# Attention with relative bias and a maxout FFN: row pairs from (2,3) on, and DMA transposes of q and k at later places

## The chip, the cores and the metric

The kernel runs on one core of a Trainium2 chip. The core has a matrix engine (TensorE, PE in the profile; its weight loads are PEld), a vector engine (VectorE, DVE), an activation engine (ScalarE, ACT), GpSimd (POOL), SyncE (SP), which issues transfers, and 16 DMA engines, which carry out what SP, POOL and ACT issue. The engines run their instructions in order, each by itself, and wait for one another by semaphores. The metric is the time of one execution on the device, in microseconds (us); less is better.

## The reference

```python
batch, n_heads, seq, head_dim = (8, 8, 576, 64)
scores = scale * np.matmul(q, k.transpose(0, 1, 3, 2))
scores = scores + bias.transpose(2, 0, 1)[None, :, :, :]   # bias by distance, 32 buckets
attn = np.exp(scores - max); attn = attn / (sum + 1e-09)
x = np.matmul(attn, v)  ->  (4608, 512): tokens x all heads
h = np.maximum(np.maximum(x @ w1, x @ w2), x @ w3)         # 512 -> 768
out = h @ w_out                                            # 768 -> 512
```

Eight batches of eight heads, 576 tokens each, give 4608 tokens of 512 numbers; each goes through three products, their maximum, and one product more.

## The kernel before

**Visits.** The kernel works through batch indices b = 0 to 7 and, in each, through four head pairs hp = 0 to 3; one step (b,hp) is called a visit here. A visit computes the scores of its two heads transposed, keys on the 128 partitions: four key tiles of 128 (tiles `sc`), and the 64 left-over keys and queries (`sct`, `scq`). ScalarE takes the exponential into `e` (main) and `el` (left over), and VectorE multiplies by a band of exponentials of the bias (`hank`, `bandt`). The weighted sum over v (tile `a`) of a visit stands in the next visit, since its exponentials have to be there; VectorE divides it by the sums (`rd`, `x_sb`). After the last head pair of a batch five DMA transposes bring `x_sb` into `xT`, as the FFN needs it.

**The FFN beside it.** The FFN of 512 tokens is cut into stages, one for each of four visits: from (b,2) on, (b,2), (b,3) and (b+1,0) each compute the first two products for two of six blocks of 128 hidden units and the third product of the two blocks before; (b+1,1) computes three of four output tiles, (b+1,2) the fourth. For batch indices below 2 and in the end the FFN is woven in otherwise.

**Two forms of a visit.** In a *plain* visit (tiled, but not rows) scores come in groups of 256 columns, the left-over keys and the weighted sum use the whole array (128 rows), and the gates use two 64-row tiles with a bank for each output. In a *row* visit everything is made of pairs of matmuls on the two 64-row halves of the array, in two passes with the operands swapped (`rows(False)`, `rows(True)`), with tiles two banks wide; the second pass waits for a semaphore that the end of the first raises. Scores come as `key_scores` of 512 columns, one key tile at a time, and the first one of a visit is computed at the end of the visit before (`ahead`). The constant ROWS (line 64) says with which visit the row form begins. There the banks are allotted anew (lines 1219 to 1223) and the visit computes its first two key tiles itself (`lead`, line 1232). The stages of the FFN of batch b - 1 are planned at (b,1) with the same constant (line 1348): the form of a stage is that of its visit.

**Loads and transposes.** GpSimd's queue loads q and k with a cast to bf16, by head pair: pairs 0 and 1 and the left-over rows of batch b + 2 at the end of (b,1) (`begin_qk`, line 1361), pairs 2 and 3 of b + 1 and its v just ahead of them. From batch 2 on, SyncE's queue transposes them into `qT` and `kT` by DMA, five steps a batch of two transposes (q and k) each: pair 0, the left-over rows (`left`, out of `qtail` and `ktail`), pairs 1, 2 and 3. The function `transposes` (line 724) gives this list; the table `places` (lines 1198 to 1200) says at which place (b, hp, half of the visit) each is put into SyncE's program, and `turn_ahead` (line 1202) does it. The same queue carries the output stores (`store_outputs`) and the transposes of `x_sb` (line 1021), in program order. qT, kT and the load tiles have two buffers, for alternate batches.

A name's first part says what it is in the profile: `psp` are gates, thirds and outputs in pairs of halves, `ps` in the whole array, `pso` outputs, `m` and `hT` the running maximum, `osb` an output tile. All matmuls are recorded at line 109; exponentials at 827; DMA transposes of q and k at 731 (pairs) and 738 (left-over rows).

Of the kernel before, what the change touches and what calls it, by code (L numbers as in the profile page):

```python
# [39 lines left out]
def kernel(  # L40
# [20 lines left out]
    QS = 2 * P  # L61
    QM = 2 * QS
    KT = 4
    ROWS = (3, 0)
    DEEP = 6
    PACKETS = 6 * QM
    FCH = d_ff // P
# [32 lines left out]
    def free_banks():  # L100
        ps_f.release()
        ps_a.release()
# [1094 lines left out]
    turns = {n: [] for n in range(2, B)}  # L1197
    places = {2: ((1, 1, 0), (1, 1, 1), (1, 2, 0), (1, 3, 1), (2, 1, 0)), 3: ((2, 2, 0), (2, 2, 1), (2, 3, 0), (3, 0, 0), (3, 0, 1))}
    for n in range(4, B):
        places[n] = tuple((n - 1, hp, half) for hp, half in ((1, 0), (1, 1), (2, 0), (2, 1), (3, 0)))  # L1200

    def turn_ahead(*place):

# [7 lines left out]
    for b, hp in [(b, hp) for b in range(1, B) for hp in range(HP)]:  # L1211
# [5 lines left out]
        tiled = bool(stages)  # L1217
        rows = (b, hp) >= ROWS
        if (b, hp) == ROWS:
            free_banks()  # L1220
# [124 lines left out]
        if hp == 1 and b > 1:  # L1345
            pending.extend((n, [fn]) for n, fn in rest)
            rest.clear()
            made, tail = ffn((b - 1) * CH, CH, False, [(b + (i + 2) // HP, (i + 2) % HP) >= ROWS for i in range(HP)])
        if hp == 1 and b + 1 < B:
# [23 lines left out]
        if hp == 1 and b > 1:  # L1373
            stages.extend(made)
            strict.append(b)
        if ROWS <= divmod(HP * b + hp + 1, HP) < (B, 0):
            late.append(lambda b=b, hp=hp, e4=e4, el=el: attend_rows(b, hp, e4, el))
# [53 lines left out]
```

## Time and profile before

| | us |
|---|---|
| median of 3 runs | 306.69 |
| lowest and highest run | 306.29, 310.19 |
| span of the profiled execution | 305.2 |
| idle time of TensorE from 88.20 to 96.63 (visit (3,0)) | 8.43 - 8.01 = 0.42 |
| the same from 151.91 to 159.70 (visit (5,0)) | 0.00 |

The profile is of one execution; its own time as a run is not recorded beside its span, from its first instruction to its last. Views used here are the page (busy time of each engine, and the span in 40 slices, each digit the busy share in tenths), the chain of work that ended last (start, duration, what), the waits by engine (total, times, longest) and the timeline: start, duration, engine, line, operation, output<-inputs, form, count, and in brackets the idle time before it with what ended it. A q behind an engine's name is its queue: the instruction only issues a transfer, which lands later. "64*128" in a matmul's form is a half of the array, "128*128" the whole.

### The profile page before, as it was taken

How to read it: one execution, taken by the hardware profiler on the slowest of the kernel's cores; microseconds unless marked ns; L12 is line 12 of the kernel's file. 1: busy time of each engine (PE TensorE's matmuls, PEld its weight loads, DVE VectorE, ACT ScalarE, POOL GpSimd, SP SyncE). 2: the span in 40 equal slices, each digit the busy share in tenths (PEclk: the TensorE clock that was granted, in tenths of full speed). 3: DMA queues.
4: the chain of work that ended last, by engine and by line, in shares of the span. 5: the costliest groups of instructions: out<-in, count | busy, mean ns of one | idle time of the engine just before them, and what ended most of it. 6: DMA issues, size and time to landing. Idle time of an engine off the chain costs nothing.

```text
span 305.2 us, 11001 instructions
## 1 busy us (share of the span) xinstructions
PE 295.5 (97%) x4745; PEld 183.7 (60%) x4745; DVE 206.3 (68%) x455; ACT 201.3 (66%) x270; POOL 143.7 (47%) x199
## 2 busy tenths in 40 slices
PE   8789999999999999999999999999999999999995
PEld 2367877765656676567666766676667654444442
DVE  6489888777776677676777677767776765453552
ACT  3999988977786787768776877677777720222211
POOL 8989677725839746774676469462000000000000
PEclk9999999999999999999999999999999999999999
DMA  9999999999999999999999999999623013202003
GB/s 160 187 203 194 176 137 120 114 165 128 223 150 121 150 131 205 174 143 192 181 139 135 202 162 146 138 197 171 79 46 140 6 40 94 84 0 108 31 0 137
DMA packets 165776, 40.51 MB, mean 133 GB/s; under 512 B 154584, under 2 KB 161248, under 8 KB 165728
## 3 DMA queue, kind: packets, MB, share of 16 engines
q0 software_dynamic: 105664, 16.66, 95.5%
q1 hardware_dynamic: 58304, 22.69, 41.6%
q8 instruction: 37, 0.61, 0.8%
q10 hardware_dynamic: 1760, 0.47, 0.7%
q14 instruction: 11, 0.09, 0.1%
HBM read 35.39 MB, written 9.45 MB: 147 GB/s over the span
## 4 chain that ended last, share of the span: by engine, by line
PE 80%; ACT 7%; DMA 6%; DVE 3%; SPq 2%; issue 1%; DVEq 0%; ACTq 0%
PE psp L109 32%; PE ps L109 15%; PE a L109 12%; PE sc L109 8%; PE pso L109 6%; ACT e L827 5%; DMA kT<-ktail 5%; PE sct L109 2%; PE warm L109 1%; PE scq L109 1%; ACT el L827 1%; SPq L738 1%; SPq L731 1%; DVE e L807 1%; DMA out_dram<-osb 1%
## 5 line engine op out<-in xcount | busy, mean ns | idle before, releaser
L827 ACT ACTIVATE e<-sc 128x1024 bf16<-128x1024 f32 x128 | 129.0, 1026 | 29.3 <-PE sc L109 28.0
L109 PEld LDWEIGHTS <-w_bf 64*128 64x128 bf16 (+1 forms) x1112 | 75.8, 95 | 55.3 <-issue 1.9
L109 PE MATMUL psp<-xT,w_bf 64*128 64x512 bf16 x784 | 97.2, 376 | 0.0
L807 DVE TENSOR_TENSOR e<-e,hank 128x512 bf16<-128x512 bf16 (+2 forms) x120 | 56.1, 473 | 13.9 <-ACT e L827 13.2
L109 PE MATMUL ps<-xT,w_bf 128*128 128x512 bf16 (+1 forms) x328 | 59.1, 332 | 0.0
L109 PE MATMUL sc<-qT,kT 64*128 64x256 bf16 (+1 forms) x352 | 48.5, 319 | 2.3 <-ACT e L827 1.1
L109 PEld LDWEIGHTS <-kT 64*128 64x128 bf16 (+1 forms) x712 | 30.0, 94 | 24.8 <-issue 6.8
L109 PE MATMUL a<-vx,e 64*128 64x65 bf16 (+1 forms) x1664 | 44.9, 190 | 0.0
L199 POOL DMA_DIRECT2D k_sb<-in_k_dram x48 | 36.2, 764 | 17.8 <-DMA vx<-in_v_dram 7.8
L199 POOL DMA_DIRECT2D q_sb<-in_q_dram x48 | 36.4, 767 | 15.1 <-DMA vx<-in_v_dram 5.7
L109 PEld LDWEIGHTS <-e 64*128 64x128 bf16 (+1 forms) x1664 | 40.8, 95 | 4.3
L109 PEld LDWEIGHTS <-hT 64*128 64x128 bf16 (+1 forms) x462 | 28.3, 95 | 18.7 <-DVE hT L551 1.6
L167 POOL DMA_DIRECT2D vx<-in_v_dram x28 | 24.8, 893 | 19.5 <-PE a L109 5.4
L109 PE MATMUL psp<-wo_bf,hT 64*128 64x256 bf16 (+1 forms) x360 | 31.7, 305 | 0.0
L421 ACT ACTIVATE m<-ps 128x512 bf16<-128x512 f32 x14 | 8.4, 597 | 34.3 <-PE ps L109 34.3
L827 ACT ACTIVATE el<-sct 128x576 bf16<-128x576 f32 (+2 forms) x36 | 21.7, 605 | 14.0 <-PE sct L109 13.9
L109 PEld LDWEIGHTS <-el 64*128 64x128 bf16 (+1 forms) x676 | 26.4, 94 | 7.0 <-issue 4.4
L109 PE MATMUL a<-vt,el 64*128 64x65 bf16 (+1 forms) x260 | 29.5, 198 | 0.2 <-DVE m L511 0.2
L551 DVE TENSOR_TENSOR hT<-psp,m 128x1024 bf16<-128x1024 f32 (+1 forms) x20 | 18.7, 956 | 9.1 <-PE psp L109 9.1
L109 PE MATMUL pso<-wo_bf,hT 128*128 128x512 bf16 (+2 forms) x102 | 21.7, 366 | 0.0
L430 DVE TENSOR_TENSOR m<-ps,m 128x512 bf16<-128x512 f32 x14 | 9.7, 692 | 17.0 <-PE ps L109 17.0
L537 DVE TENSOR_TENSOR m<-psp,m 128x1024 bf16<-128x1024 f32 x15 | 18.4, 1225 | 3.3 <-PE psp L109 3.1
(82 smaller groups left out, 292.8 us busy)
## 6 DMA issues: line engine op xcount, KB each, us to landing
out_dram<-osb SPq DMA_DIRECT2D x35, 256.0 KB, 4.7
vx<-in_v_dram POOLq DMA_DIRECT2D x28, 128.0 KB, 6.7
q_sb<-in_q_dram POOLq DMA_DIRECT2D x50, 64.0 KB, 5.3
k_sb<-in_k_dram POOLq DMA_DIRECT2D x48, 64.0 KB, 5.3
w_bf<-in_moe_w_dram POOLq DMA_DIRECT2D x2, 512.0 KB, 8.5
xT<-in_k_dram SPq DMA_DIRECT2D x6, 128.0 KB, 4.5
hank<-w_dr SPq DMA_DIRECT2D x2, 384.0 KB, 5.7
w_bf<-in_moe_w_dram POOLq DMA_DIRECT2D x1, 768.0 KB, 8.1
```

The lines of the kernel that those rows point to most:

```text
L109: made = inorder(nc.tensor.matmul(*args, **kw))
L167: in_turn(b, nc.gpsimd.dma_start(out=dst[:, t, h0:h1, :], in_=x[:, t, h0:h1, :]), P * (h1 - h0))
L199: in_turn(b, nc.gpsimd.dma_start(out=dst[:, g, :, par, :], in_=part), KT * P)
L421: nc.scalar.activation(out=st[fb]["m0"][:], in_=ps0, func=ACTF.Copy)
L430: inorder(nc.vector.tensor_tensor(out=m[:], in0=ps1, in1=st[fb]["m0"][:], op=ALU.max))
L537: return lambda: inorder(nc.vector.tensor_tensor(out=m[0][:], in0=ps1(), in1=m[0][:], op=ALU.max,))
L551: inorder(nc.vector.tensor_tensor(out=out_[:, i : i + n], in0=ps2()[:, i : i + n], in1=m[0][:, i : i + n], op=ALU.max,))
L731: inorder(nc.sync.dma_start_transpose(out=made[j][:, g, 0 : KT * P].rearrange("p (t n) -> p t n", t=KT), in_=batch[b][j][:, g].rearrange(" ...
L738: inorder(nc.sync.dma_start_transpose(out=made[j][:, :, KT * P : KT * P + n], in_=(qtail, ktail)[j][b % 2][0:n].rearrange("p h c -> p (h c)"),
L807: put(nc.vector.tensor_tensor(out=e4[:, t, :, lo:hi], in0=e4[:, t, :, lo:hi], in1=hank[:, 2 * hp : 2 * hp + 2, c0:c1][:, :, ::-1], op=ALU. ...
L827: made = nc.scalar.activation(out=out_, in_=in_, func=ACTF.Exp, scale=inv_sqrt_d)
```

## The change

```diff
-    ROWS = (3, 0)
+    ROWS = (2, 3)
...
     places = {2: ((1, 1, 0), (1, 1, 1), (1, 2, 0), (1, 3, 1), (2, 1, 0)), 3: ((2, 2, 0), (2, 2, 1), (2, 3, 0), (3, 0, 0), (3, 0, 1))}
     for n in range(4, B):
-        places[n] = tuple((n - 1, hp, half) for hp, half in ((1, 0), (1, 1), (2, 0), (2, 1), (3, 0)))
+        places[n] = ((n - 1, 1, 1), (n - 1, 2, 0), (n - 1, 2, 1), (n, 0, 0), (n, 1, 0))
```

The row form begins one visit sooner, with (2,3). And from batch 4 on each of the five steps is put into SyncE's program one place later or more: pair 0 at the second half of (n-1,1), the left-over rows and pair 1 in (n-1,2), pair 2 only at the start of (n,0) and pair 3 at the start of (n,1), in the batch that uses them. Batches 2 and 3 keep their places.

TensorE at the start of (2,3), before: the end of the second score group, then the weighted sum of (2,2) (tile a) on the whole array.

```order
L109 LDWEIGHTS kT_924
L109 MATMUL sc_1844<-qT_923,kT_924 128x256
L109 LDWEIGHTS el_1677
L109 MATMUL a_1852<-vt0_95,el_1677 128x130
L109 LDWEIGHTS e4_1676
L109 MATMUL a_1852<-vx0_93,e4_1676 128x65
```

And now, at the same place:

```order
L109 LDWEIGHTS kT_924
L109 MATMUL sc_1850<-qT_923,kT_924 128x512
L109 LDWEIGHTS el_1677
L109 MATMUL a_1854<-vt0_95,el_1677 128x65
L109 LDWEIGHTS el_1677
L109 MATMUL a_1854<-vt0_95,el_1677 128x65
L109 LDWEIGHTS e4_1676
L109 MATMUL a_1854<-vx0_93,e4_1676 128x65
```

Scores are now whole key tiles of 512 columns, and the sum's matmuls come in pairs, one for each half of the array.

SyncE's queue around (4,0), before (qT_2306, kT_2307 are batch 4, x_sb_1992 batch 3, qT_3161, kT_3162 batch 5; osb are stores): pairs 2 and 3 of batch 4, x of batch 3, pair 0 of batch 5, three stores, the left-over rows of batch 5.

```order
L731 DMA_TRANSPOSE kT_2307<-k_sb_1642 128x4x128
L731 DMA_TRANSPOSE qT_2306<-q_sb_1641 128x4x128
L731 DMA_TRANSPOSE kT_2307<-k_sb_1642 128x4x128
L1021 DMA_TRANSPOSE xT_101<-x_sb_1992 128x4x128 x4
L1021 DMA_TRANSPOSE xT_101<-x_sb_1992 128x4x64
L731 DMA_TRANSPOSE qT_3161<-q_sb_2448 128x4x128
L731 DMA_TRANSPOSE kT_3162<-k_sb_2449 128x4x128
L579 DMA out_0_dram<-osb_3259 128x512
L579 DMA out_0_dram<-osb_3267 128x512
L579 DMA out_0_dram<-osb_3281 128x512
L738 DMA_TRANSPOSE qT_3161<-qtail1_98 128x4x64
```

And now (qT_2467, kT_2468 are batch 4, x_sb_2046 batch 3, qT_3322, kT_3323 batch 5):

```order
L731 DMA_TRANSPOSE kT_2468<-k_sb_1642 128x4x128
L1021 DMA_TRANSPOSE xT_101<-x_sb_2046 128x4x128 x4
L1021 DMA_TRANSPOSE xT_101<-x_sb_2046 128x4x64
L731 DMA_TRANSPOSE qT_2467<-q_sb_1641 128x4x128
L731 DMA_TRANSPOSE kT_2468<-k_sb_1642 128x4x128
L579 DMA out_0_dram<-osb_3295 128x512
L579 DMA out_0_dram<-osb_3303 128x512
L579 DMA out_0_dram<-osb_3317 128x512
L731 DMA_TRANSPOSE qT_3322<-q_sb_2486 128x4x128
L731 DMA_TRANSPOSE kT_3323<-k_sb_2487 128x4x128
L738 DMA_TRANSPOSE qT_3322<-qtail1_98 128x4x64
```

x of batch 3 has moved ahead of pair 3 of batch 4, and the three stores ahead of pair 0 of batch 5. The order on GpSimd's queue is the same as before.

## The prediction

> I write (b,hp) for the visit of batch index b and head pair hp, and "left 4", "pair 0 of batch 4" for the two DMA transposes (of q, then of k) that bring the left-over rows or a head pair of that batch.
>
> **What bounds the kernel now.** I read the page first: engine shares, the slices, then the chain of work that ended last; then the waits of TensorE; then the timeline of TensorE and of SyncE's queue around the places that the change touches.
>
> ```profile
> span 305.2 us, 11001 instructions
> PE 295.5 (97%) x4745; PEld 183.7 (60%) x4745; DVE 206.3 (68%) x455; ACT 201.3 (66%) x270; POOL 143.7 (47%) x199
> PE   8789999999999999999999999999999999999995
> DMA  9999999999999999999999999999623013202003
> ```
>
> TensorE is busy in every slice, so only less work or fewer bubbles on it shorten the span. The DMA engines are full until about slice 28 (214 us), so a transpose shares them with loads. The waits of TensorE and the chain name the one DMA that matters:
>
> ```profile
> PE sct L109 <- DMA kT<-ktail: 0.6, 2, 0.3
> ...
> 82.17 8.31 DMA kT<-ktail
> ...
> 115.26 6.87 DMA kT<-ktail
> ```
>
> TensorE waits twice for a transpose of left-over keys: left 3, issued at 82.17 and landed 8.31 later at 90.48, and left 4, landed at 122.13. The waits themselves are short (0.6 us together), but both landings lie on the chain: TensorE cannot pass them, however early it arrives. After 122 us no wait for a transpose is left.
>
> **The change, first part: (2,3) becomes a visit in row pairs.** These rows are the plain (2,3), the old first row visit (3,0) and its end:
>
> ```profile
> 79.29 0.62 PE L109 MATMUL sc<-qT,kT 64*128 64x256 bf16 x8
> 79.84 0.23 PE L109 MATMUL a<-vt,el 128*128 128x130 bf16 x1
> ...
> 88.20 0.21 PE L109 MATMUL a<-vt,el 64*128 64x65 bf16 x2 [0.17 <-DVE m L511]
> ...
> 89.89 0.29 PE L109 MATMUL a<-vx,el 64*128 64x65 bf16 x8
> 90.53 0.30 PE L109 MATMUL sct<-qT,kT 64*128 64x288 bf16 x2 [0.35 <-DMA kT<-ktail]
> ...
> 96.63 0.21 PE L109 MATMUL a<-vt,el 64*128 64x65 bf16 x2
> ```
>
> From the first weighted sum of one visit to that of the next, (2,3) takes 88.20 - 79.84 = 8.36 us and (3,0) takes 96.63 - 88.20 = 8.43. A settled row visit, (5,0), looks so:
>
> ```profile
> 151.91 0.21 PE L109 MATMUL a<-vt,el 64*128 64x65 bf16 x2
> ...
> 153.50 0.29 PE L109 MATMUL sct<-qT,kT 64*128 64x288 bf16 x2
> ...
> 159.70 0.21 PE L109 MATMUL a<-vt,el 64*128 64x65 bf16 x2
> ```
>
> It takes 7.79 us: 1.59 to its left-over keys (sct), then 6.20. On paper 8.36 + 8.43 - 2 x 7.79 = 1.2 us lie in these two visits, less the cost of entering the row scheme, which moves to (2,3) and does not vanish. I lay the new order on these durations:
>
> - (2,3) now enters. Its scores start at 79.29 as before. Its first weighted sum needs the two-bank tile, and so the vector maximum that frees the old bank:
>
> ```profile
> 79.32 0.69 DVE L511 TENSOR_TENSOR m<-psp,m 128x512 bf16<-128x512 f32 x1
> ```
>
>  It ends at 80.01; the same wait in (3,0) was followed by TensorE 0.05 later, so the sum starts at 80.06 (0.22 later than before).
> - From there to the last group of the second rows is 89.89 - 88.20 = 1.69, and 0.12 more is its own step: 81.87 for the left-over keys of batch 2, which landed long ago. Then 96.63 - 90.53 = 6.10, as in the old entering visit: (3,0) starts its weighted sum at 87.97. That is 0.23 sooner than 88.20, with one score tile of (3,0) done where two were before.
> - (3,0), now settled, wants its left-over keys 1.59 later, at 89.56. But left 3 lands at 90.48, if SyncE issues it when it did:
>
> ```profile
> 73.55 1.19 SPq L731 DMA_TRANSPOSE kT<-k_sb  x1
> ...
> 80.25 0.53 SPq L465 DMA_DIRECT2D out_dram<-osb  x1
> 80.88 1.19 SPq L738 DMA_TRANSPOSE qT<-qtail  x1
> 82.17 1.26 SPq L738 DMA_TRANSPOSE kT<-ktail  x1
> ```
>
>  SyncE's order up to here is not changed, nor GpSimd's, and from 73.55 (a wait for a load) to 82.17 its queue runs back to back, without waiting for TensorE. So the keys start at 90.53 again, after a wait of 0.97 in place of 0.35, and 6.20 later, at 96.73, stands (3,1): 0.10 later than before. The gain of the row visit is eaten by a DMA.
>
> The matmul work itself is nearly the same (the same 16 + 8 gate products per visit; scores of 4 x 512 columns a head in either form). The two changes of tile form that (2,3) loses (into 128 rows at 79.84, and back) cost 79.84 - 79.29 - 0.44 = 0.11 us for the first, if two score groups stream for twice the 0.22 of one tile; they are inside the visit times above, so nothing is added. [...]
>
> **Second part: the transposes from batch 4 on.** SyncE's new order for batch b is: pair 2 of b, x of b-1 (five transposes), pair 3 of b, three stores, pair 0 of b+1, left b+1, one store, pair 1 of b+1. Transposes and stores are the same ones; only their order changes. I check each date against the rows.
>
> ```profile
> 107.08 1.20 SPq L731 DMA_TRANSPOSE kT<-k_sb  x1
> 108.84 1.21 SPq L731 DMA_TRANSPOSE qT<-q_sb  x1
> 110.16 1.96 SPq L731 DMA_TRANSPOSE kT<-k_sb  x1
> 112.22 1.57 SPq L579 DMA_DIRECT2D out_dram<-osb  x3
> 113.88 1.28 SPq L738 DMA_TRANSPOSE qT<-qtail  x1
> ...
> 119.08 0.40 PE L109 MATMUL sc<-qT,kT 64*128 64x512 bf16 x2
> ...
> 122.18 0.29 PE L109 MATMUL sct<-qT,kT 64*128 64x288 bf16 x2 [0.26 <-DMA kT<-ktail]
> ```
>
> - Batch 4, pair 0 now goes behind the three stores: the issues keep their sum, so pair 0 slips by the stores' 1.57 (its k from 110.16 to about 111.7) and left 4 stays at 113.88 / 115.26. Left 4 then lands at 122.13 again and the keys of (4,0) start at 122.18, whatever TensorE gained or lost before: the 0.10 from above is gone too. Cost 0.
> - Pair 0's k landed 6.4 after its issue: 118.1 against its first use at 119.08. Over the run the latency of the transposes to kT is
>
> ```profile
> DMA to landing us min/median/max: 2.3/5.9/8.3
> ```
>
>  so with the longest, 8.3, it would land at 120.0 and hold TensorE for 0.9 us, of which the 0.26 that left 4 cost is given back: 0 to +0.7; I take 0, since the row that is moved itself shows 6.4.
> - From batch 5 on the slack is wide:
>
> ```profile
> 136.87 0.69 DVE L126 COPY osb<-psp 128x512 f32<-128x512 f32 x1 [0.19 <-PE psp L109]
> ...
> 150.83 0.40 PE L109 MATMUL sc<-qT,kT 64*128 64x512 bf16 x2
> ...
> 122.25 0.82 DVE L1013 TENSOR_TENSOR x_sb<-a,rd 128x640 bf16<-128x640 f32 x1
> ...
> 129.41 7.00 SPq L1021 DMA_TRANSPOSE xT<-x_sb  x5
> ...
> 143.03 0.40 PE L109 MATMUL sc<-qT,kT 64*128 64x512 bf16 x2
> ...
> 152.12 0.79 POOL L199 DMA_DIRECT2D q_sb<-in_q_dram  x1
> ```
>
>  The last output of (4,1) is ready at 137.56; stores and pair 0 of batch 5 follow, its k issued by 140; even with 8.3 it lands at 148.3, before 150.83. The x transposes of batch 3 no longer stand behind pair 3: ready at 123.07, they run to about 130.5, and pair 3 of batch 4 follows, k at 132, landed by 140.3 at 8.3, before its first use at 143.03. TensorE waited for no x transpose before, so their 6 us earlier buy nothing: 0.
> - GpSimd's loads for batch b+2 overwrite what pair 3 of b reads. Those of batch 6 start at 152.12; pair 3 of batch 4 is done at 140. 12 us of cover: 0.
>
> **Sum.** +0.10 at (3,0), taken back at (4,0) by the same landing as before, 0 after it: the span stays 305.2. The profiled execution's own time isn't shown beside its span; the median of the three runs is 306.69, 1.5 above it. I predict 306.7.
>
> **Rivals.**
> - *The gain gets through (faster).* If left 3 lands by 89.5 and left 4 by 121, both 1 us earlier than in the rows, the 0.97 wait goes, (3,1) stands at 95.77, and (4,0) saves the 0.43 between 122.18 and 120.16 + 1.59 as well: 0.86 + 0.43 = 1.3 us, 305.4. For it: latencies run from 2.3 to 8.3 and left 3's 8.3 is the longest. Against: nothing ahead of left 3 changes on SyncE or GpSimd.
> - *Pair 0 of batch 4 misses its date (slower).* Place (3,3), decided once its latency exceeds 119.08 - 111.7 = 7.4; at 8.3 and with pair 3 of batch 3 equally unlucky (it lands at 110.85, used at 111.28) I price it at 1 us: 307.7. [...]
> - *Own-batch transposes come late each time (clearly slower).* One mechanism: pair 3 behind the five x transposes, in (4,1) to (7,1). It decides when x ends 2.7 us later than the 130.5 above (143.03 - 140.3). Each 2 us missed costs 2 in four batches: 314.7. Against: x needs only rows of the same visit, and its own 7.00 us are in the row.
>
> **Chances and range.** Forecast (pinned by left 3 and left 4) 0.74; gain gets through 0.12; pair 0 late 0.10; own-batch transposes late each time 0.04. The range runs over the first three: from 305.3 to 308.4, the top being 307.7 with what the runs before differ by (306.29 to 306.69, and one at 310.19). A difference under 2% (6.1 us) cannot be told from no change here. Faster by over 2% would need 300.6, below every case: 0.01. Slower by over 2% is the last case: 0.04. Within: 0.95.
>
> **What would show it.** In the profile after: the keys of (3,0) still wait for left 3 at about 90.5, now about 1 us; (4,0)'s keys start near 122.2; settled visits keep 7.79; no wait of TensorE for pair 0 to 3. Wrong would be: a wait `sc <- DMA kT` or `qT` at (3,3) or later, left 3 landing elsewhere than at 90.5, or (2,3) not near 7.9 us.

## The result and the profile after

| | before | after |
|---|---|---|
| median of 20 runs each (us) | 307.30 | 308.95 |
| lowest and highest run (us) | 306.26, 310.19 | 306.99, 311.44 |
| after to before | | 1.0055, interval 1.0033 to 1.0077 |
| profiled execution: span (its own time) | 305.2 | 308.8 (310.58) |

Ratios and intervals, here and below, leave out executions over 1.5% above the fastest of their kernel (one of e1, two of e4, one of before beside e9 to e12), which the medians keep.

The changed kernel is 1.65 us slower by the medians, half a per cent: little, but outside what I predicted. The kernel before, at 307.30 in 20 runs, lies 0.61 above the 306.69 of the 3 runs that the forecast started from. The profiled execution after is one of the slower of its kernel, so its 3.6 us over the one before must be taken apart by place before anything is blamed on the change. First the page of after (span; busy time and share of the engines; the busy tenths of TensorE and its granted clock in 40 slices), then the waits of TensorE (total, times, longest):

```profile
span 308.8 us, 11086 instructions
PE 296.3 (96%) x4784; PEld 185.2 (60%) x4792; DVE 206.4 (67%) x451; ACT 201.1 (65%) x269; POOL 143.4 (46%) x199
PE   8868999999999999999999998999999999999995
PEclk9997999999999999999999999999999999999999
```

```profile
PE xp L113 <- DVE qT L126: 1.9, 1, 1.9
PE psp L109 <- issue: 1.4, 1, 1.4
...
PE a L109 <- DVE m L511: 0.2, 1, 0.2
```

No wait for a DMA transpose is left on TensorE. Two waits are new, and neither was in the prediction: one for VectorE early on, and one "issue", a time in which TensorE waited for nothing that the profile shows. The windows of after show by visit where time went (from the first weighted sum of a visit to that of the next; length, then busy time and count of each engine, the granted clock behind POOL's count):

```profile
74.92:82.85 7.93, 7.71 (x107) 4.40 (x106) 5.44 (x15) 6.18 (x9) 5.36 (x7) 1.00 1.84 205
82.85:90.86 8.01, 7.94 (x156) 4.90 (x157) 5.32 (x11) 6.15 (x9) 5.46 (x8) 1.00 1.84 165
90.86:98.66 7.80, 7.80 (x161) 4.94 (x158) 5.57 (x10) 5.97 (x8) 6.65 (x10) 1.00 2.14 150
177.29:185.09 7.80, 7.80 (x161) 5.12 (x159) 5.57 (x10) 5.96 (x8) 5.84 (x9) 1.00 2.03 165
185.09:194.64 9.55, 8.16 (x160) 5.38 (x158) 5.58 (x10) 5.96 (x8) 5.04 (x7) 1.00 2.24 145
```

These are (2,2), (2,3), (3,0), (5,3) and (6,0). The same for (2,2), (2,3) and (3,0) before:

```profile
72.05:79.84 7.79, 7.79 (x112) 4.75 (x110) 5.21 (x14) 5.99 (x8) 5.13 (x8) 1.00 1.97 190
79.84:88.20 8.36, 8.19 (x110) 4.59 (x109) 6.28 (x16) 6.40 (x10) 5.30 (x7) 1.00 1.99 189
88.20:96.63 8.43, 8.01 (x156) 4.82 (x157) 5.33 (x11) 6.15 (x9) 6.23 (x9) 1.00 1.69 134
```

The 3.6 us between the two profiles split into three places:

- **Up to (2,2): +2.87** (74.92 against 72.05). Both kernels run the same program there. The windows from 23.7 to 27.2, of after and then of before, show a clock of 0.51 in after where before has 1.00; ahead of it stands the 1.9 us wait for VectorE.

```profile
23.70:27.20 3.50, 3.25 (x37) 2.14 (x37) 3.10 (x12) 1.58 (x3) 3.36 (x5) 0.51 1.55 192
```

```profile
23.70:27.20 3.50, 3.32 (x70) 2.45 (x67) 3.43 (x12) 3.50 (x7) 3.37 (x5) 1.00 1.50 198
```

- **Where the change acts, a gain: -1.28.** (2,2), (2,3), (3,0) and (4,0) took 7.79 + 8.36 + 8.43 + 8.23 = 32.81 before and 7.93 + 8.01 + 7.80 + 7.79 = 31.53 after. The visit in row form is shorter, and both waits for left-over keys are gone; how little of that the change itself earns is said further down.
- **Later, a loss: +2.03.** (5,0) takes 8.06 and (6,0) takes 9.55 in place of 7.79. The timeline of TensorE in (6,0) shows the stall:

```profile
186.56 0.29 PE L109 MATMUL a<-vx,el 64*128 64x65 bf16 x8
186.68 0.30 PE L109 MATMUL sct<-qT,kT 64*128 64x288 bf16 x2
186.80 0.59 PE L109 MATMUL psp<-xT,w_bf 64*128 64x512 bf16 x3
188.78 0.82 PE L109 MATMUL psp<-xT,w_bf 64*128 64x512 bf16 x5 [1.39 <-issue]
```

The run of eight gate products that stands behind `sct` breaks off after three, though its operands are the ones that the first three used. I read this as TensorE lacking its own next instructions. The page's table of DMA queues (packets, MB, share of 16 engines) lists an instruction queue, and its packets in the window from 186.2 to 187.3 are the second row:

```profile
q8 instruction: 37, 0.61, 0.8%
...
q8 instruction: 1, 0.02, 5.4%
```

0.61 MB in 37 packets are 16 KB each; over some 9,580 matmuls and weight loads that is about 64 bytes for one, so by this estimate a packet holds 256 of them. (The page of e9 below, whose kernel has 256 matmuls and weight loads more than the one before, shows 38 packets in place of 37, and 0.62 MB, so I take the queue to be TensorE's.) In the trace this one lands at 187.23, and 1.55 us later TensorE goes on. Counting every recorded instruction of TensorE, its few semaphore instructions too, the one that came late is no. 6592 = 25 x 256 + 192. So my reading is that the instructions come in over this queue during the execution, 256 at a time, and that TensorE stood still here for 1.39 us because a packet came late.

That gives the theory tested below. The change makes TensorE's program 94 instructions longer (47 matmuls and 47 weight loads in (2,3); the page of after lacks some matmul records, but e9 below, with 81 more, has 4873 matmuls against 4745 before, and 4873 - 4745 - 81 is 47). By the theory everything behind it moves against the blocks of 256, and a block boundary comes to lie where its fetch is late.

### The profile page after: what moved, and what is told of

It is laid out like the page before. It is cut to its first block, busy times and chain, and to the rows that moved or that the text cites. A ratio compares the mean times of both kernels' runs of the same rounds, so it can differ in the third digit from the quotient of the medians.

```text
span 308.8 us, 11086 instructions
## 1 busy us (share of the span) xinstructions
PE 296.3 (96%) x4784; PEld 185.2 (60%) x4792; DVE 206.4 (67%) x451; ACT 201.1 (65%) x269; POOL 143.4 (46%) x199
## 4 chain that ended last, share of the span: by engine, by line
PE 87%; ACT 5%; DVE 4%; issue 2%; DMA 1%; DVEq 0%; ACTq 0%
PE psp L109 37%; PE ps L109 16%; PE a L109 14%; PE sc L109 9%; PE pso L109 6%; ACT e L827 4%; PE sct L109 2%; PE warm L109 1%; ACT el L827 1%; PE scq L109 1%; DVE e L807 1%; PE tp L113 1%; DMA out_dram<-osb 1%; DVE e L822 1%; DVE qT L126 1%
## 5 line engine op out<-in xcount | busy, mean ns | idle before, releaser
L109 PEld LDWEIGHTS <-w_bf 64*128 64x128 bf16 (+1 forms) x1120 | 77.0, 95 | 57.0 <-issue 4.4
L109 PE MATMUL psp<-xT,w_bf 64*128 64x512 bf16 x800 | 99.9, 376 | 1.4 <-issue 1.4
L807 DVE TENSOR_TENSOR e<-e,hank 128x512 bf16<-128x512 bf16 (+2 forms) x120 | 57.3, 483 | 13.2 <-ACT e L827 12.5
L109 PE MATMUL ps<-xT,w_bf 128*128 128x512 bf16 (+1 forms) x317 | 56.9, 331 | 0.2
L109 PE MATMUL sc<-qT,kT 64*128 64x256 bf16 (+1 forms) x344 | 49.7, 326 | 2.3 <-ACT e L827 1.0
L551 DVE TENSOR_TENSOR hT<-psp,m 128x1024 bf16<-128x1024 f32 (+1 forms) x21 | 19.9, 968 | 10.7 <-PE psp L109 10.7
L537 DVE TENSOR_TENSOR m<-psp,m 128x1024 bf16<-128x1024 f32 x16 | 19.6, 1224 | 3.5 <-PE psp L109 3.4
```

What stands on the lines that cost most here:

```text
L109: made = inorder(nc.tensor.matmul(*args, **kw))
L537: return lambda: inorder(nc.vector.tensor_tensor(out=m[0][:], in0=ps1(), in1=m[0][:], op=ALU.max,))
L551: inorder(nc.vector.tensor_tensor(out=out_[:, i : i + n], in0=ps2()[:, i : i + n], in1=m[0][:, i : i + n], op=ALU.max,))
L807: put(nc.vector.tensor_tensor(out=e4[:, t, :, lo:hi], in0=e4[:, t, :, lo:hi], in1=hank[:, 2 * hp : 2 * hp + 2, c0:c1][:, :, ::-1], op=ALU. ...
```

## The experiments

I call the *position of after* the one with 94 more instructions ahead of the stages from (2,3) on, and the *position of before* the one with a multiple of 256 more (0 or 256). Tiny matmuls put ahead of the first weighted sums, in the warm-up, move the position without touching a visit:

```diff
         on_zeros(idle[:], n)
...
+        for _ in range(PADS.pop(0)):
+            mm(idle[0:8, 0:8], lhsT=zeros[:, 0:8], rhs=zeros[:, 0:8])
...
+    PADS = [11, 12, 12, 12]
```

These four numbers sum to 47 matmuls, 94 instructions; [20, 20, 20, 21] give 162, which with the change's 94 make 256; four times 32 give 256. In the padded kernels (2,2) starts at the same time as in others within what those vary (71.8 to 74.4 us).

**e1: the changed kernel once more.**

> The changed kernel once more, for a second profile. Theory F (instruction fetch): TensorE stalls on its own next instructions (a wait put down to 'issue' of 0.5 us or more) at one or two 16 KB refills of the run, at other visits than in the first profile; ratio to before 1.003 to 1.008. Theory T (late transposes): waits of TensorE for qT or kT appear instead. If neither shows in the settled visits and the ratio is still 1.005, the loss lies ahead of (2,2), where the program is the same, and something else must be found.

308.84 us, 1.0037 (1.0009 to 1.0065). The early loss is not there: (2,2) starts at 72.10, and no VectorE wait over 1.2 us. The stall is, at another block (7616 = 29 x 256 + 192), in (6,3), as the timeline of e1 shows:

```profile
208.39 0.59 PE L109 MATMUL psp<-xT,w_bf 64*128 64x512 bf16 x3
210.10 1.68 PE L109 MATMUL psp<-xT,w_bf 64*128 64x512 bf16 x13 [1.12 <-issue]
```

So the early loss is a draw of one execution, and the stall stays, as theory F had it.

**e2 and e3: each part alone.** e2 has only the first line of the change, e3 only the second (the table `places`); e2's diff is

```diff
-    ROWS = (3, 0)
+    ROWS = (2, 3)
```

> Only the first part: row form from (2,3) on, old places. Theory F with the places as the cause: 0.998 to 1.002, (2,3) near 8.0 us and (3,0) near 7.8 to 8.4. Rival R (the row form itself, or the 85 instructions that it adds to TensorE's program, makes the refills late): 1.003 to 1.008, with an issue stall in the settled visits.

> Only the second part: later places from batch 4 on, row form from (3,0) as before. Theory F with the places as the cause: 1.003 to 1.008. Rival R: 0.998 to 1.002.

e2: 308.97 us, 1.0069 (1.0039 to 1.0098), with a stall in (6,3) (9.36 in place of 7.80). e3: 307.61, 1.0015 (0.9982 to 1.0049), no stall from (4,0) on. The loss comes with ROWS, the part that lengthens TensorE's program, as rival R had it, and what the later transposes cost alone can't be told from nothing. (The 85 of the expectation is the difference of all recorded instructions; TensorE's program grows by 94.)

**e4: both parts, but pairs 2 and 3 transposed a batch ahead, in (n-1,3).**

```diff
+        places[n] = ((n - 1, 1, 1), (n - 1, 2, 0), (n - 1, 2, 1), (n - 1, 3, 0), (n - 1, 3, 1))
```

> Both parts, but pairs 2 and 3 stay in the batch before (third head pair's visit), so that the transposes of x follow them again as in the old order. If the five x transposes now issued right behind pair 2 at the start of each batch are what fills the DMA rings when a refill is due, this comes back to 0.998 to 1.002; if the later pair 0, left-over rows and pair 1 are the cause, it stays at 1.003 to 1.008; under rival R it stays at 1.003 to 1.008 as well.

309.35, 1.0059 (1.0025 to 1.0093), with (6,0) and (6,3) longer by 0.68 and 0.99 (waits on issue of 0.3 and 0.6). The own-batch transposes are not the cause.

**e5, e12: the kernel before at the position of after** (94 tiny).

> The kernel before with 47 tiny matmuls (94 instructions of TensorE, as many as the change adds) beside the first four visits, results unused. Theory P (phase: TensorE's program is fetched in blocks of 256 instructions; 94 more instructions move the block borders so that a short block meets slow transfers around the start of each batch): 1.002 to 1.008, and a wait put down to issue of 0.5 us or more near a visit (b,0) in most profiles, though neither part of the change is in it. Rival R2 (the row form at (2,3) itself, by what it does on the engines): 0.999 to 1.002, no issue wait.

> e5 once more, for its interval (1.0016, 0.9988 to 1.0044): the kernel before with 47 tiny matmuls, at the blocks of 256 as after. Position theory: 1.002 to 1.006 and a stall of 0.5 to 1.5 us at the start of one or two (b,0). Rival: 0.998 to 1.002.

307.67, 1.0016 (0.9988 to 1.0044), and 307.50, 1.0015 (0.9986 to 1.0044). The stall came both times where the theory has it, in (6,0); the waits of TensorE in e12:

```profile
PE psp L109 <- issue: 0.6, 1, 0.6
```

(6,0) took 8.86 and 8.77 in place of 7.79. In time, though, neither run can be told from no change: the ratios fall where the rivals put them.

**e6, e10: the changed kernel at the position of before** (162 tiny).

> The changed kernel with 81 tiny matmuls (162 instructions; 94 + 162 = 256, so the block borders stand again where they stand in the kernel before). Theory P: 0.993 to 0.999, no issue wait over 0.4 us in the row visits, and the visits (2,2) to (3,0) about 1 us shorter than before. Rival R2: 1.003 to 1.008 as the changed kernel.

> e6 once more, for its interval (1.0026, 1.0000 to 1.0052). Position theory: 1.000 to 1.004 and no stall of over 0.3 us at the start of a (b,0). Rival, the change itself costs time: 1.003 to 1.007.

307.91, 1.0026 (1.0000 to 1.0052), and 308.41, 1.0030 (0.9997 to 1.0064). No wait on issue from (4,0) on in either, but ahead of it they are not free of them; the waits of TensorE in e6, and then in e10:

```profile
PE a L109 <- issue: 0.8, 2, 0.6
```

```profile
PE a L109 <- issue: 0.6, 1, 0.6
```

Those of e6 stand at 67.56 and 114.98 (in (3,3), which lost 0.77), that of e10 at 68.76. Ahead of (2,3) these two kernels lie 162 instructions further on than before, which is neither position; but in (3,3) e6 is at the position of before, and e3 has a wait there too, of 0.2. In time they decide little: e6 misses the 0.993 to 0.999 of theory P and lies just below the rival's range, and e10's 1.0030 lies in both.

**e7, e8: before and after with 256 tiny, positions kept.** They show what the padding itself costs.

> Control: the kernel before with 128 tiny matmuls (256 instructions, one whole block, so the borders keep their places). Theory P: 0.998 to 1.002, plus at most 1 us if the tiny matmuls themselves hold up the first visits (then seen ahead of 20 us). If the tiny matmuls cost as such, e7 is slower than e5.

> Control on the other side: the changed kernel with 128 tiny matmuls (one whole block). Theory P: 1.003 to 1.008 as the changed kernel, with an issue wait near a visit (b,0); against e6 it is slower by 1 to 3 us although both differ from the changed kernel by tiny matmuls alone. Rival R2: the same as e6.

307.96, 1.0043 (1.0013 to 1.0073), no stall from (4,0) on; and 309.11, 1.0057 (1.0028 to 1.0087), (6,0) and (6,3) longer by 0.64 and 0.67 (waits on issue of 0.3 each). Padding by 256 isn't free: the first weighted sum comes at 19.05 and 18.64, in the unpadded kernels at 17.80 to 18.03, and with 94 or 162 at 17.33 to 18.11. Where the position is that of after, the stall is back, and e8 is 1.2 us slower than e6, as theory P had it.

**e9: ROWS alone at the position of before** (162 tiny). This is e2 moved by padding, by more work and not less.

> Row pairs from (2,3) with the places of before, and 81 tiny matmuls (162 instructions of TensorE) ahead of the first weighted sums: TensorE's program then stands at the blocks of 256 as the kernel before does, with everything else as in e2. If the position in the blocks is what made e2 slower (1.0069), no stall of TensorE on issue at (b,0) and a ratio of 0.998 to 1.004. If ROWS by itself costs time in another way, 1.004 to 1.009 again.

307.13, 1.0005 (0.9974 to 1.0035), against e2's 1.0069 (1.0039 to 1.0098): the intervals do not meet. Its waits of TensorE have no "issue" row, its windows for (2,2), (2,3), (3,0) and (6,0) keep the gain and show no stall, and on the timeline the eight gate products that broke off in after run through:

```profile
71.75:79.68 7.93, 7.76 (x108) 4.40 (x106) 5.45 (x15) 6.19 (x9) 6.26 (x9) 1.00 1.95 228
79.68:87.69 8.01, 7.94 (x156) 4.91 (x157) 5.32 (x11) 6.15 (x9) 4.37 (x6) 1.00 1.82 178
87.69:95.60 7.91, 7.91 (x161) 5.02 (x158) 5.58 (x10) 5.96 (x8) 5.28 (x8) 1.00 1.62 105
181.73:189.53 7.80, 7.80 (x161) 4.94 (x159) 5.58 (x10) 5.97 (x8) 6.68 (x10) 1.00 2.08 138
```

```profile
183.32 0.30 PE L109 MATMUL sct<-qT,kT 64*128 64x288 bf16 x2
183.44 1.04 PE L109 MATMUL psp<-xT,w_bf 64*128 64x512 bf16 x8
```

**e11: places alone at the position of after** (94 tiny).

> The places of after with ROWS of before, and 47 tiny matmuls (94 instructions), so that TensorE's program stands at the blocks of 256 as after does. Position theory: a stall of 0.5 to 1.5 us on issue in psp at the start of one or two of the visits (5,0) to (7,0), and a ratio of 1.002 to 1.007. Rival, the position matters little: 0.999 to 1.003 as e3 (1.0015).

308.48, 1.0040 (1.0014 to 1.0065), and the stall in (6,0), again after three of eight, both as the position theory had them:

```profile
184.72 0.59 PE L109 MATMUL psp<-xT,w_bf 64*128 64x512 bf16 x3
186.67 0.82 PE L109 MATMUL psp<-xT,w_bf 64*128 64x512 bf16 x5 [1.36 <-issue]
```

**All profiles together.** "Stretch" runs from the first weighted sum of (2,2) to that behind (7,3); "lost from (4,1) on" sums what its visits took beyond the usual 7.79, 8.35, 7.37 and 7.80.

| kernel | position | stretch (us) | lost from (4,1) on (us) | ratio |
|---|---|---|---|---|
| before | before | 173.80 | 0.0 | 1 |
| e3 places | before | 173.21 | 0.0 | 1.0015 |
| e7 before + 256 | before | 173.04 | 0.0 | 1.0043 |
| e6, e10 after + 162 | before | 173.32, 172.59 | 0.0, 0.1 | 1.0026, 1.0030 |
| e9 rows + 162 | before | 172.62 | 0.0 | 1.0005 |
| after, e1 | after | 174.57, 173.98 | 2.1, 1.5 | 1.0055, 1.0037 |
| e2 rows | after | 174.08 | 1.6 | 1.0069 |
| e4 | after | 174.17 | 1.7 | 1.0059 |
| e8 after + 256 | after | 173.80 | 1.3 | 1.0057 |
| e5, e12 before + 94 | after | 173.89, 174.26 | 1.1, 1.0 | 1.0016, 1.0015 |
| e11 places + 94 | after | 174.91 | 1.8 | 1.0040 |

All eight profiles at the position of after have a stall on instructions from (4,1) on, and lose 1.0 to 2.1 us there; none of the six at the position of before has one there. All fourteen profiles together have fourteen waits on issue: these ten, and four that the column doesn't count, of 0.2 to 0.6, in e3, e6 and e10. (The column leaves out (3,3) too, which is 0.2 to 0.8 longer than its 7.80 in e3, e6 and e7.) By the count used above all fourteen fall at no. 191 to 195 of a block of 256, and each ends 1.25 to 1.55 us after a packet of the instruction queue has landed. So where the stalls come is shown.

What they cost in time is shown less well. after, e1, e2 and e4, 49 runs, each taken against the median of before beside it, have a median of 1.0058 (1.0043 to 1.0069, by resampling); e6, e9 and e10, 36 runs with the new ROWS at the position of before, have 1.0026 (1.0007 to 1.0042). The difference, 0.32% (0.10 to 0.53), is 1.0 us, about the size of the stalls. With the old ROWS no such difference is seen: e5, e11 and e12, 36 runs at the position of after, have 1.0024, and e3 and e7, 24 runs at that of before, have 1.0024 as well (difference 0.01%, -0.25 to 0.17), though the profiles of the first three lose 1.0 to 1.8 us. That pair isn't clean, since e7 pays some 1 us for its own padding (e3 alone has 1.0016), but it gives the stalls no support.

What stays open: how much of the 1.65 us is the stall. From (2,2) on, after, e1, e2, e4 and e8 take 0.0 to 0.8 us more than the one profile of before, and 0.6 to 1.5 more than e3 and e7, which have the old ROWS and position and no wait for left-over keys. What is left would lie ahead of (2,2), where one execution differs from the next by more than that (behind (7,3) all take 59.3). The early drop of the clock is not it: without the three runs of after with a recorded clock below 0.996, its median is 308.88. And e6 and e10 lie some 0.3% above before though their stretch is shorter; their small waits on issue and the early draw (e10's profile has a VectorE wait of 1.8 us) may be part of that, but e9 has the same padding and none of the loss. One profile a run doesn't settle it. No version here beats the kernel before: the best, e9, equals it.

## Why the prediction missed

The forecast was 306.7 us, 305.3 to 308.4; the kernel takes 308.95. Of these 2.25 us 0.61 is the base, from 3 runs. The step that failed for the rest is the count of the change's work: I called the matmul work "nearly the same", and took it that from batch 5 on nothing changes for TensorE. The busy time is nearly the same, but the program is 94 instructions longer, and (5,0) and (6,0) of the profile after took 2.03 us more, by the reading above through where the program lies in the blocks of 256; the sum had 0 there. No rival held this.

- **(2,3) as a row visit, from 80.06 to 87.97 = 7.91:** it took 8.01 in all changed kernels, and (2,2) 7.92 with its later end: right within 0.1 to 0.2.
- **"(3,0) wants left 3 at 89.56, left 3 lands at 90.48 again":** wrong, and this was the step that made the gain zero. The sizes of one profile were taken as dates. SyncE's queue in after, with the issue of left 3, and the latency that the DMA view gives for it there and, second, in e1:

```profile
83.05 1.22 SPq L738 DMA_TRANSPOSE kT<-ktail  x1
...
kT<-ktail SPq DMA_TRANSPOSE x1, 6.8
```

```profile
79.13 1.26 SPq L738 DMA_TRANSPOSE kT<-ktail  x1
...
kT<-ktail SPq DMA_TRANSPOSE x1, 8.3
```

 In after it landed at 89.9, and (3,0)'s keys, at 92.45, did not wait. In e1 TensorE reached (2,2) at 72.10, as before (72.05), but left 3 was issued 3.04 us sooner (79.13, not 82.17) and landed at 87.4 in spite of the same 8.3 of latency. Both issue and latency vary from one execution to the next. Nor does SyncE's queue run "without waiting for TensorE" there: in after an earlier transpose of q holds it for 3.36 us, against 1.23 before (at 77.56), and SyncE's waits from 68 to 86 us put this down to TensorE:

```profile
76.29 3.36 SPq L731 DMA_TRANSPOSE qT<-q_sb  x1
...
SPq L731 <- PE scq L109: 3.2, 1, 3.2
```

 Among six profiles with ROWS as before (before, e3, e5, e7, e11, e12) TensorE waits for it only in before and e12 (0.2 us), so what the row visit is worth without that wait is less: 7.69 + 8.36 + 8.01 + 7.79 = 31.85 in e7 against 31.53 in after, 0.3 us.
- **Left 4 at 122.13, (4,0) pinned again:** wrong in the same way. In after it was issued at 113.19, landed at 117.84, and (4,0) took 7.79.
- **Pair 0 of batch 4 and all transposes from batch 5 on cost 0:** right. No wait for `qT` or `kT` by DMA in after, and e3 alone is 1.0015 (0.9982 to 1.0049).
- **Settled visits keep 7.79:** right for most, wrong for (6,0), through the stall, and for (5,0), where TensorE goes on 1.42 us after a packet of the same queue has landed.
- **The rivals:** the gain did get through (1.28 us against the 1.3 of that rival), but most of it is waits for left-over keys that before's own profile happened to have, and it is not what the time shows. The pair 0 rival gave 307.7 for a wait that never came.
- **The range:** that a difference under 2% can't be told from no change was wrong: 20 runs each tell 0.55% apart. The top was the pair 0 rival plus the spread of two runs (whose 0.40 gives 308.1, not 308.4). It held no cost for the program's position, and none for the early part, which moves (2,2) by up to 2.9 us between executions of the same code (after and e1).

## What to carry to other kernels

Here an edit that added 94 instructions to some 9,490 moved all later ones against blocks of 256 (as estimated above), and all eight profiles at the position of after have waits on issue of 0.3 to 1.4 us from (4,1) on. Where TensorE is busy as it was here (296.3 of 308.8 us in after), look for waits on "issue" inside a run of equal matmuls, and compare with a padded kernel before crediting or blaming the edit itself. A landing read from one profile is one draw: before using it as the date that pins a chain, ask what sets its issue, and give the case in which it comes sooner a real chance. Where a profiled run lies far from its median, split the difference by place first; what stands ahead of the change is not its doing.

## What the runs showed of the hardware

- **TensorE stood still at one place in its blocks.** The fourteen waits on issue, of 0.2 to 1.4 us, are all at no. 191 to 195 of 256, and in all fourteen TensorE goes on 1.25 to 1.55 us after a packet of the instruction queue has landed; that it had run out of instructions is my reading of this. In after, the fetch that landed at 187.23 began 3.9 us after TensorE had entered the block before (at 182.40) and took 0.94; TensorE was through that block in 4.6 us, since the weighted sum ahead of the stall issues some 180 instructions in 1.6 us. In e9 the boundary nearest by falls elsewhere: the block wanted at 181.94 was in by 178.12. Why a fetch starts late isn't settled. From 186.2 to 187.3 the profile of after has the packets of queues q0 and q1 at 166.1% and 33.9% of 16 engines' time, and the one packet of q8 at 5.4%; whether the first two held up the third was not tried.
- **The first stage differed between two executions.** With the same code one waits 1.9 us for VectorE near 22 us and then runs 3.5 us at a granted clock of 0.51 (after); the other has no such wait over 1.2 us, and a clock of 1.00 in the same window (e1). What sets it off was not tried.
